# Recurrence and token mixing on one core: four-token rows for keys and receptances, a two-bank product without drains, a new written order

## The chip, the cores and the metric

The kernel runs on one core of one Trainium2 chip. The metric is the device time of one execution in microseconds. The page of the profile names the engines PE (TensorE products), PEld (its weight loads), DVE (VectorE), ACT (ScalarE), POOL (GpSimd) and SP (SyncE, which issues the DMAs).

## The reference

Two stages follow each other, for 4 batches, 8 heads, 768 tokens and 48 columns a head. Arrays r, k, v, w are [4, 8, 768, 48] in float32; u is [8, 48].

```python
for t in range(S):                      # a recurrence over tokens, one 48x48 state a head
    cur = einsum('bhd,bhe->bhde', u[None] * kt, vt)          # the bonus of the token itself
    y[:, :, t] = einsum('bhd,bhde->bhe', rt, state + cur)
    state = wt[:, :, :, None] * state + einsum('bhd,bhe->bhde', kt, vt)
...
x = y as [4, 768, 384]
W_tok = scale * einsum('bsd,btd->bst', x @ w_q, x @ w_k)     # w_q, w_k: [384, 64]
out = maximum(einsum('bst,btd->bsd', W_tok, x), 0) @ w_out   # w_out: [384, 384]
```

## The kernel before, in words

The 768 tokens of a batch are cut into chunks of 128 tokens (C) and the work into units of two chunks (U = 256 tokens, all 8 heads). There are N = 12 units, three a batch. A unit loads its decays (wg), keys (kg), receptances (rg) and values (vg), 384 KB each, with `load` (L299): a partition holds two neighbouring tokens of every head, so a row in DRAM that is moved at a time is 2 x 48 floats, 384 bytes, and one DMA fills 128 partitions. For the last batch (WHOLE) the values of all three units come through `load_whole` (L304) in four DMAs of 64 partitions with rows of 192 bytes.

Within a unit the steps are these; the names in brackets are the tiles of the profile.

- ScalarE takes the logarithm of the decays (lw); GpSimd or ScalarE casts keys and receptances to bf16 (k, r), GpSimd the values (v).
- PE sums the logarithms over the tokens of a chunk with a triangle of ones (CM); ScalarE makes exp of the sum (ep, `f_ep` L497, one instruction a unit) and of its negative (en, `f_en` L502). In the first and the last unit this goes chunk by chunk.
- PE transposes keys and receptances (`transposed` L513). VectorE or ScalarE copies the transposed keys (ks); VectorE makes receptances times ep (RT) and receptances times keys (qT). Keys times en (KT, `f_KT` L550) is GpSimd's, except in the first and last unit, where VectorE reads the keys from PSUM.
- The values go through PE to put the tokens of a chunk on the partitions in the order of the transposed keys (v times PM or ID16), and are copied (VB). With the bonus vector UB a product gives a number a token and head (dd), GpSimd multiplies it into the values (Vd).
- Within a chunk: KT times RT (PE), times a mask on VectorE (AM, 128x1024, once a chunk), times VB (`f_ya`).
- Between chunks: keys transposed back (kd), the state of a head pair grown on PE and scaled on VectorE (SB), and RT times the old state, `f_yi` (L717). [...] The step goes in "sides": first the even heads of chunk 0 with the odd heads of chunk 1, then the other two, and ahead of a second side stands a drain of PE:

```python
sides = [[(0, 0), (1, 1)], [(1, 0), (0, 1)]]      # pairs (chunk, odd or even head)
...
if not first:
    nc.tensor.drain()
```

- Both results of a chunk lie in one PSUM bank; VectorE scales by gx and adds Vd in one instruction for the two chunks (X, `f_x` L751).
- X is transposed (XT) and multiplied by w_q and w_k (QK). After the third unit of a batch, T sums keys times X over the tokens, and each unit of the batch is finished: QK times TS, relu (MX), times w_out (wo), copy (os), store.

All PSUM is one tile of eight banks. `unit` (L436) does not issue instructions; it adds steps to `Plan` with an engine or a choice of engines, a duration in ns, the steps it comes after, and the buffers that it fills and reads. `Plan.order` (L86) walks these steps as a list scheduler: on each engine they stand by a written rank (RANK, L171), choices between engines come from a string (ALT, L205), and a PSUM bank is chosen where a buffer comes free. The program is issued in the order that comes out; nothing reorders it later. Loads go to SP's queue in that order; rings of four tiles for wg, kg, rg and vg hold them, so a load waits until the cast of the unit four before it is done. `mm` (L247) is the helper through which every product goes, so all PE instructions stand on L248 in the profile; `copy` is on L391 to L399.

Of the kernel before, what the change touches and what calls it, by code (L numbers as in the profile page):

```python
# [10 lines left out]
F32 = mybir.dt.float32  # L11
# [12 lines left out]
class Buf:  # L24


    def __init__(self, kind):
        self.kind = kind
        self.readers = []
        self.filler = None  # L30
        self.bank = None


class Plan:
# [3 lines left out]
    SWITCH = 93  # L38
    LAND = 1950

    def __init__(self, rings, alt):
        self.rings = rings
        self.alt = iter(alt)
        self.last = {}
        self.steps = []

    def add(self, key, engs, fn, after=(), buf=None, reads=(), lag=None, mode=0, behind=None):
        opts = {}
        for e, x in engs.items():
            x = x if isinstance(x, tuple) else (x, mode, None)  # L50
            own = (260 if e in "Ee" else 80) if lag is None else lag
            opts[e] = (e.upper(), x[0], own, x[1], x[2])
        e = next(iter(opts)) if len(opts) == 1 else next(self.alt, "")
        e = e if e in opts else next(iter(opts))
        eng, dur, own, mode, kind = opts[e]
        if kind is not None:
            buf.kind = kind
        s = dict(key=key, opts=opts, way=e, eng=eng, dur=dur, fn=fn, lag=own, mode=mode, rank=0,
                 behind=behind, after=list(after), buf=buf, reads=list(reads), i=len(self.steps))
        if buf is not None:  # L60
            if buf.filler is None:
                buf.filler = s
                s["fill"] = buf.kind
                if behind is None:
                    s["behind"] = self.last.get(buf.kind)
                if buf.kind in self.rings:
                    self.last[buf.kind] = s
            else:
                s["fill"] = None
                if behind is None:  # L70
                    s["behind"] = buf.filler
        else:
            s["fill"] = None
        for b in reads:
            b.readers.append(s)
        self.steps.append(s)
        return s

    def dma(self, key, issue, dur, fn, after=(), buf=None, reads=(), behind=None):

        i = self.add(key, {"S": issue}, fn, after, buf, lag=0, behind=behind)
        m = self.add(key + ("wire",), {"Q": dur}, None, [i], lag=0)
        l = self.add(key + ("land",), {"L": self.LAND}, None, [m], lag=0, reads=reads)
        return i, l

    def order(self):  # L86
        never = 1 << 60
        queues = {e: [] for e in "EADPS"}
        for s in sorted(self.steps, key=lambda s: s["rank"]):
            if s["eng"] in queues:  # L90
                queues[s["eng"]].append(s)
        wires = {}
        for s in self.steps:
            if s["eng"] in "QL":
                wires.setdefault(s["after"][0]["i"], s)
        free = dict.fromkeys("EADPSQ", 0)
        place = dict.fromkeys("EADPS", 0)
        rings = {k: [] for k in self.rings}
        owners, moved, done, mode = [None] * 8, [], [], 0

        def clear(b):
            if b is None:
                return 0
            return max([x.get("end", never) for x in b.readers], default=0)

        def start(s):
            if any("end" not in a for a in s["after"]):
                return never, None
            t = max([free[s["eng"]]] + [a["end"] for a in s["after"]])
            if s["behind"] is not None:  # L110
                if "start" not in s["behind"]:
                    return never, None
                t = max(t, s["behind"]["start"])
            if s["eng"] == "S" and len(moved) >= 3:
                t = max(t, moved[-3])
            if s["fill"] in ("w", "s"):
                two = s["fill"] == "w"
                at = [clear(x) for x in owners]
                end = 7 if two else 8
                t = max(t, min(max(at[x:x + 1 + two]) for x in range(end)))  # L120
                if t >= never:
                    return never, None

                def beside(x):
                    return (x > 0 and at[x - 1] <= t) + (x < end - 1 and at[x + 1 + two] <= t)
                x = min((x for x in range(end) if max(at[x:x + 1 + two]) <= t),
                        key=lambda x: (beside(x), x if two else -x))
                return t, (x, 1 + two)
            if s["fill"] is not None:
                ring, size = rings[s["fill"]], self.rings[s["fill"]]  # L130
                if len(ring) >= size:
                    t = max(t, clear(ring[-size]))
            return t, None

        def run(s, t, took):
            s["start"], s["end"] = t, t + took + s["lag"]
            free[s["eng"]] = t + took
            done.append(s)

        while True:  # L140
            heads = [(start(q[place[e]]), e) for e, q in queues.items() if place[e] < len(q)]
            if not heads:
                break
            (t, at), e = min(heads, key=lambda h: h[0][0])
            assert t < never, "the plan is stuck"
            s = queues[e][place[e]]
            place[e] += 1
            if at is not None:
                s["buf"].bank = at[0]
                for x in range(at[0], sum(at)):  # L150
                    owners[x] = s["buf"]
            elif s["fill"] is not None:
                rings[s["fill"]].append(s["buf"])
            change = e == "E" and s["mode"] != mode
            if e == "E":
                mode = s["mode"]
            run(s, t, s["dur"] + self.SWITCH * change)
            if s["i"] in wires:
                m = wires[s["i"]]
                run(m, max(free["Q"], s["end"]), m["dur"])  # L160
                moved.append(free["Q"])
                x = wires[m["i"]]
                x["start"], x["end"] = m["end"], m["end"] + x["dur"]
                done.append(x)
        assert len(done) == len(self.steps)
        return done

RANK = [  # L171
# [40 lines left out]
def kernel(  # L212
# [24 lines left out]
    HW = H * D2  # L237
    N = B * NU

    WHOLE = (3,)  # L240
    DIRECT = (0, N - 1)

    SHIFT = 25
# [690 lines left out]
```

## Time and profile before

| | |
|---|---|
| runs | 106.45, 120.07, 106.38 us; median 106.45 |
| profiled execution, span | 104.5 us, from its first to its last instruction; mean granted clock 0.955 |
| busy PE, DVE, ACT, POOL | 88.3, 81.7, 81.0, 69.8 us |
| DMA | 24.68 MB in 56805 packets, 54480 of them under 512 bytes |
| granted clock of PE | half from 20.1 to 26.9 us and in the last 2 us |
| first load landed, waited for by ACT | 4.47 us |
| cast of the last receptances (POOL) | 79.43 us |
| last transposes of receptances on PE | 81.41 us |
| last product on PE begins / last store issued | 97.28 us (a run of 15, 2.60 us) / 100.8 us |

The page's second part cuts the span into 40 slices of 2.6 us. A line of the groups gives line, engine, operation, tiles and shape, the count, then busy us and the mean ns of one, then the idle time of the engine just ahead of them and who ended it. "issue" means that nothing which the profile shows ended a wait. In the chain in order of time each line has start, length and what ran; SPq is the issuing of a DMA on SP.

### The profile page before, as it was taken

The page shows a single profiled execution, that of the slowest core. Times are in us where ns is not written, and L with a number is a line of the kernel's source. Part 1 is how long each engine was busy: PE and PEld are TensorE (multiplying, and loading weights), DVE is VectorE, ACT ScalarE, POOL GpSimd, SP SyncE. Part 2 cuts the span into 40 slices and gives each one's busy share as a digit, 9 for nine tenths or more (in the row PEclk, how much of TensorE's full clock was granted, in tenths as well). Part 3 has the DMA queues.
Part 4 walks back from the last instruction along what each step waited for, and adds up shares of the span by engine and source line. Part 5 has one row for each costly group of instructions (what it writes and reads, how often), then busy time and mean ns, then how long its engine had stood idle before and what let it go on. Part 6 is the DMA issues. An engine that isn't in the chain of part 4 may idle for free.

```text
span 104.5 us, 4513 instructions
## 1 busy us (share of the span) xinstructions
PE 88.3 (84%) x1913; PEld 65.1 (62%) x1916; DVE 81.7 (78%) x139; ACT 81.0 (78%) x123; POOL 69.8 (67%) x80
## 2 busy tenths in 40 slices
PE   5966985589878898999899999699999999999920
PEld 2243754478756676586667777477788668866600
DVE  6628989765899797988889979989999898864500
ACT  6256999568889976987998988979889778666930
POOL 6667395998699977996876999994899506000000
PEclk9999999855899999999999999999999999999995
DMA  1999998999899999999999999999960019303792
GB/s 19 295 324 325 325 321 222 267 239 319 194 335 276 244 245 252 294 262 288 301 274 280 310 306 266 170 197 231 307 220 8 6 65 391 153 9 152 295 365 94
DMA packets 56805, 24.68 MB, mean 236 GB/s; under 512 B 54480, under 2 KB 55632, under 8 KB 56784
## 3 DMA queue, kind: packets, MB, share of 16 engines
q1 hardware_dynamic: 56224, 24.19, 83.9%
q8 instruction: 15, 0.25, 0.9%
q10 hardware_dynamic: 560, 0.20, 0.7%
q14 instruction: 6, 0.05, 0.2%
HBM read 19.66 MB, written 4.72 MB: 233 GB/s over the span
## 4 chain that ended last, share of the span: by engine, by line
PE 53%; DVE 15%; SPq 10%; DMA 6%; issue 4%; POOL 3%; ACT 3%; DVEq 0%; POOLq 0%; ACTq 0%
PE PS L248 53%; SPq L300 10%; DVE AM L636 6%; DMA kg<-in_k_dram 6%; DVE X L752 3%; DVE ks L397 3%; POOL KT L558 2%; ACT os L391 2%; POOL k L470 1%; ACT MX L403 1%; ACT VB L391 1%; DVE SB L694 1%; DVE qT L534 1%; DVE RT L548 1%; DVE XT L397 1%
## 5 line engine op out<-in xcount | busy, mean ns | idle before, releaser
L636 DVE TENSOR_TENSOR AM<-PS,US 128x1024 bf16<-128x1024 f32 x24 | 29.2, 1219 | 1.0 <-PE PS L248 0.8
L558 POOL TENSOR_TENSOR KT<-ks,en 128x1024 bf16<-128x1024 bf16 x9 | 19.1, 2127 | 5.4 <-DVE ks L397 2.4
L616 POOL TENSOR_TENSOR Vd<-VB,dd 128x768 bf16<-128x768 bf16 (+1 forms) x14 | 18.5, 1327 | 5.5 <-DVE AM L636 4.3
L752 DVE SCALAR_TENSOR_TENSOR X<-PS,gx,Vd 128x768 bf16<-128x768 f32 (+1 forms) x13 | 12.4, 953 | 2.3 <-PE PS L248 1.8
L498 ACT ACTIVATE ep<-PS 128x1024 bf16<-128x1024 f32 (+1 forms) x14 | 12.8, 922 | 1.8 <-PE PS L248 1.7
L248 PE MATMUL PS<-wo,MX 128*128 128x384 bf16 x72 | 13.2, 326 | 0.0
L503 ACT ACTIVATE en<-PS 128x1024 bf16<-128x1024 f32 (+1 forms) x14 | 12.5, 903 | 0.7 <-issue 0.4
L460 ACT ACTIVATE lw<-wg 128x768 bf16<-128x768 f32 x12 | 10.2, 847 | 2.9 <-DMA wg<-in_w_dram 2.9
L470 POOL CAST k<-kg 128x768 bf16<-128x768 f32 x12 | 9.9, 822 | 2.9 <-DMA kg<-in_k_dram 2.9
L248 PEld LDWEIGHTS <-KT 48*128 48x128 bf16 (+1 forms) x320 | 9.4, 95 | 3.4 <-issue 1.4
L391 ACT COPY os<-PS 128x768 f32<-128x768 f32 (+1 forms) x14 | 9.5, 684 | 1.4 <-PE PS L248 1.3
L403 ACT ACTIVATE MX<-PS 128x768 bf16<-128x768 f32 (+1 forms) x11 | 8.3, 754 | 2.4 <-PE PS L248 2.3
L248 PE MATMUL PS<-RT,KT 48*128 48x128 bf16 x192 | 9.7, 220 | 0.5 <-POOL KT L558 0.4
L548 DVE TENSOR_TENSOR RT<-PS,ep 128x1024 bf16<-128x1024 bf16 (+1 forms) x14 | 8.4, 609 | 1.7 <-PE PS L248 1.6
L248 PEld LDWEIGHTS <-MX 128*128 128x128 bf16 x72 | 6.5, 98 | 4.0 <-issue 0.2
L470 POOL CAST r<-rg 128x768 bf16<-128x768 f32 x10 | 8.2, 823 | 1.1 <-DMA rg<-in_r_dram 1.1
L391 ACT CAST VB<-PS 128x768 bf16<-128x768 f32 x9 | 7.2, 800 | 2.1 <-PE PS L248 2.0
L534 DVE TENSOR_TENSOR qT<-PS,ks 128x1024 bf16<-128x1024 bf16 x12 | 8.2, 684 | 0.7 <-PE PS L248 0.7
L248 PE MATMUL PS<-SB,RT 48*128 48x48 bf16 x160 | 6.9, 184 | 2.1 <-DVE AM L636 0.9
L248 PE MATMUL PS<-VB,AM 128*128 128x48 bf16 x192 | 8.7, 186 | 0.0
L579 POOL CAST v<-vg 128x768 bf16<-128x768 f32 x9 | 7.4, 824 | 1.8 <-DMA vg<-in_v_dram 1.8
L248 PE MATMUL PS<-CM,lw 64*128 64x128 bf16 x192 | 8.4, 232 | 0.2
(83 smaller groups left out, 188.1 us busy)
## 6 DMA issues: line engine op xcount, KB each, us to landing
wg<-in_w_dram SPq DMA_DIRECT2D x12, 384.0 KB, 5.5
kg<-in_k_dram SPq DMA_DIRECT2D x12, 384.0 KB, 5.6
rg<-in_r_dram SPq DMA_DIRECT2D x12, 384.0 KB, 5.8
vg<-in_v_dram SPq DMA_DIRECT2D x9, 384.0 KB, 5.4
out_dram<-os SPq DMA_DIRECT2D x9, 384.0 KB, 3.6
vw<-in_v_dram SPq DMA_DIRECT2D x4, 288.0 KB, 5.9
out_dram<-os SPq DMA_DIRECT2D x5, 192.0 KB, 2.5
wof<-in_moe_w_out_dram SPq DMA_DIRECT2D x1, 576.0 KB, 6.0
```

Source lines behind the costliest of these rows:

```text
L248: return nc.tensor.matmul(o, l, rr, start=start, stop=stop, skip_group_check=True, is_transpose=trans)
L300: nc.sync.dma_start(out=view(tl, 0, [[D2, H], [1, D2]]), in_=ap[b, :, ds(i * U, U)].rearrange("h (p j) d -> p h (j d)", j=2))
L391: nc.scalar.copy(o, i)
L460: nc.scalar.activation(view(lw.tile, 0, [[64, H], [512, 2], [1, D]]), view(g["wg"].tile, 0, [[D2, H], [D, 2], [1, D]]), ACT.Ln, bias=0.0, ...
L470: op(view(o.tile, 0, [[64, H], [512, 2], [1, D]]), view(g[src].tile, 0, [[D2, H], [D, 2], [1, D]]))
L498: nc.scalar.activation(view(ep.tile, cs[0] * NP * EW + 66, [[EW, NP * len(cs)], [-65, 2], [1, 64]]), at(cw)[:, ds(cs[0] * 512, w_)], ACT.E ...
L503: nc.scalar.activation(en.tile[:, ds(cs[0] * 512, w_)], at(cw)[:, ds(cs[0] * 512, w_)], ACT.Exp, bias=0.0, scale=-1.0)
L548: nc.vector.tensor_tensor(o, x, y, ALU.mult)
L558: x.tensor_tensor(o, view(ks.tile, cs[0] * 512, dims), y, ALU.mult)
L616: nc.gpsimd.tensor_tensor(Vd.tile[:, cols], VB.tile[:, cols], view(dd.tile, cs[0] * H, [[1, len(cs) * H], [0, D]]), ALU.mult)
L636: AMs[c] = add(("AM", n, c), {"D": 1221}, lambda e, c=c, A=A: nc.vector.tensor_tensor(view(AM[c].tile, 0, [[C, 8], [1, C]]), view(at(A), 0 ...
L752: nc.vector.scalar_tensor_tensor(view(X.tile, (2 * i + c0) * DM, [[DM, nc_], [1, DM]]), view(at(y), 0, [[512, nc_], [1, DM]]), gx, view(Vd ...
```

## The change

- Keys and receptances of the units 1 to 11 come in rows of four tokens, 768 bytes (`load_long`): 64 partitions hold the 256 tokens of a unit for four heads, the other 64 partitions the other four heads. Each such load is two DMAs of 64 partitions. The values of the last batch come in four DMAs of 32 partitions, rows of 192 bytes as before. Decays and the other values are loaded as before.
- Tokens of a chunk stand in another order: two bits of the token number choose the group of 32. Masks (CM, US, PM), positions, casts, transposes, copies and the order in QK follow. ep is laid out in runs of 32 columns and made by two instructions, each for half the columns.
- The between-chunk product goes chunk by chunk, even and odd head in turn, even heads into one PSUM bank, odd heads into the other. Outside the last unit there is no drain; X is then read bank by bank, in two instructions. The last unit keeps one drain a chunk.
- The bonus vector is loaded in rows and transposed on PE.
- KT may be made by GpSimd, by VectorE from ks or by VectorE from PSUM, in any unit; casts, VB and Vd may go to more engines; the state product has a second form with 64 columns of weights. The pads of kd are steps of the plan; wo is loaded and cast apart from wq and wk.
- The list scheduler goes: ORDER (all 734 steps), WAYS and BANKS are written out.

```diff
+    def order(self):
+        ways = iter(WAYS)
+        for s in self.steps:
+            if len(s["ways"]) > 1:
+                s["way"] = next(ways)
...
+        for b, x in zip(self.banks, BANKS):
+            b.bank = x
...
+        for i in ORDER:
+            s = self.steps[i]
...
-    WHOLE = (3,)
-    DIRECT = (0, N - 1)
+    LONG = tuple(range(1, N))
+    WHOLE = (B - 1,)
...
+    def load_long(b, i, tl, ap):
+        for g in range(2):
+            nc.sync.dma_start(
+                out=view(tl, 0, [[2 * D2, NP], [1, 2 * D2]], p0=64 * g, pn=64),
+                in_=ap[b, ds(g * NP, NP), ds(i * U, U)].rearrange("h (p s) d -> p h (s d)", s=4))
+
     def load_whole(b, q, tl):
...
+        nc.sync.dma_start(
+            out=view(tl, 0, [[D, H * NCH], [1, D]], p0=64 * (q % 2) + 32 * (q // 2), pn=32),
+            in_=dataclasses.replace(v, offset=(b * H * S + q) * D,
+                                    ap=[[4 * D, 32], [C * D, H * NCH], [1, D]]))
...
             def f_ep(e, cs=cs, w_=w_):
-                nc.scalar.activation(
-                    view(ep.tile, cs[0] * NP * EW + 66, [[EW, NP * len(cs)], [-65, 2], [1, 64]]),
-                    at(cw)[:, ds(cs[0] * 512, w_)], ACT.Exp, bias=0.0, scale=1.0)
+                for off, step, j in ((68, 34, 0), (34, -33, 1)):
+                    nc.scalar.activation(
+                        view(ep.tile, cs[0] * NP * EW + off,
+                             [[EW, NP * len(cs)], [step, 2], [1, 32]]),
+                        view(at(cw), cs[0] * 512 + j * 64, [[C, NP * len(cs)], [32, 2], [1, 32]]),
+                        ACT.Exp, bias=0.0, scale=1.0)
...
+                if long:
+                    for hp in range(2):
+                        for s in range(4):
+                            for x in range(2):
+                                rows = ds(x * 64, 64)
+                                mm(at_long(x, place + hp * C + (s % 2) * 64 + (s // 2) * 32),
+                                   src.tile[rows, ds(s * 256 + hp * 128, 128)],
+                                   ID16[rows, rows], trans=True)
+                    return
...
+            y = add(("KT", n, cs[0]), "PDd", f_KT, [ens[c] for c in cs], KT, [en],
+                    cols=512 * len(cs), half=half,
+                    more=dict(P=([kss], [ks]), D=([kss], [ks]), d=([kTs], [kr])))
...
-        if end:
-            sides = [[(0, 0)], [(0, 1)], [(1, 1)], [(1, 0)]]
-        else:
-            sides = [[(0, 0), (1, 1)], [(1, 0), (0, 1)]]
...
+        def of(c, h):
+            return at(ys[c])[:, ds(h * D if end else h % 2 * 512 + (c * NP + h // 2) * D, D)]
+
+        def f_yi(e, c, start):
+            heads = [(hp, hh) for hp in range(NP) for hh in range(2)]
+            if end:
+                heads.sort(key=lambda x: x[1])
+            for x, (hp, hh) in enumerate(heads):
+                if end and x == NP:
+                    nc.tensor.drain()
+                mm(of(c, 2 * hp + hh), RT.tile[ds(hh * 64, D), ds((c * NP + hp) * C, C)],
+                   olds[c].tile[ds(hh * 64, D), ds(hp * D, D)],
+                   start=(start and hp == 0 and not (end and hh)), stop=False)
...
             def f_x(e, c0=c0, nc_=nc_, y=y):
-                nc.vector.scalar_tensor_tensor(
-                    view(X.tile, (2 * i + c0) * DM, [[DM, nc_], [1, DM]]),
-                    view(at(y), 0, [[512, nc_], [1, DM]]), gx,
-                    view(Vd.tile, c0 * DM, [[DM, nc_], [1, DM]]), ALU.mult, ALU.add)
+                for hh in range(2) if not end else ():
+                    nc.vector.scalar_tensor_tensor(
+                        view(X.tile, 2 * i * DM + hh * D, [[D2, H], [1, D]]),
+                        view(at(y), hh * 512, [[D, H], [1, D]]), gx,
+                        view(Vd.tile, hh * D, [[D2, H], [1, D]]), ALU.mult, ALU.add)
...
```

In SP's queue the first loads stand, before, as w0 k0 r0 v0 k1 w1 r1 v1 w2 r2 k2 v2 (the number is the unit), and after as w0 k0 r0 v0 k1 w1 r1 v1 w2 k2 r2 v2, where k1, r1, k2, r2 are two DMAs each.

More of the change, by code (lines that the diff above doesn't have):

```diff
@@ L24, with __init__, add @@
 class Buf:
-    def __init__(self, kind):
+    def __init__(self, kind, tile=None):
         self.kind = kind
-        self.readers = []
+        self.tile = tile
         self.filler = None
+        self.before = None
         self.bank = None
 class Plan:
[L38 to L44, printed above, removed]
-        self.steps = []
[L47 to L59, printed above, removed]
+    ENGINE = dict(E="E", e="E", c="E", A="A", D="D", d="D", P="P", S="S", Q="Q", L="L")
+    def __init__(self):
+        self.steps = []
+        self.banks = []
+    def add(self, key, ways, fn, after=(), buf=None, reads=(), cols=0, mode=0, behind=None,
+            half=-1, more=None):
+        s = dict(key=key, ways=ways, way=ways[0], fn=fn, after=list(after), buf=buf,
+                 reads=list(reads), cols=cols, mode=mode, behind=behind, half=half,
+                 more=more or {}, i=len(self.steps), fills=False, out=False)
         if buf is not None:
@@ L62, in add @@
                 buf.filler = s
[L63 to L67, printed above, removed]
-            else:
[L69 to L75, printed above, removed]
+                s["fills"] = True
@@ L76, in add @@
+                if buf.tile is None:
+                    self.banks.append(buf)
+                elif behind is None and buf.before is not None:
+                    s["behind"] = buf.before.filler
+            elif behind is None:
+                s["behind"] = buf.filler
         self.steps.append(s)
         return s
[L79 to L84, printed above, removed]
@@ L86, in order @@
-    def order(self):
[L87 to L92, printed above, removed]
-        for s in self.steps:
[L94 to L137, printed above, removed]
-            done.append(s)
[L140 to L165, printed above, removed]
-        return done
@@ L171 @@
-RANK = [
[32 rows of a table removed]
-]
-ALT = ("PPDEAAADeAAPADPeAAeAeAAPPDPeAAAEADAAAAAAAPADPEAAeAEDAPPADEAAEDEDAPPDPeAADEDAAAAAAAAPPAPe"
-       "ADEAeAAPPDPEAAEAEDAPPDPeAAAEDAAAAAAAAPPDPAeAEAAPPAPAEDeADPPAAAEDDDEDDAADDDAADAAADAA")
+    def order(self):
+        ways = iter(WAYS)
+        for s in self.steps:
+            if len(s["ways"]) > 1:
+                s["way"] = next(ways)
+                assert s["way"] in s["ways"], s["key"]
+            s["eng"] = self.ENGINE[s["way"]]
+        for b, x in zip(self.banks, BANKS):
+            b.bank = x
+        assert sorted(ORDER) == list(range(len(self.steps)))
+        done = []
+        for i in ORDER:
+            s = self.steps[i]
+            assert all(x["out"] for x in s["after"]), s["key"]
+            if s["buf"] is not None and s["buf"].kind == "x":
+                s["buf"].kind = "s" if s["way"] == "E" else "w"
+            s["out"] = True
+            done.append(s)
+        return done
@@ L559, in unit @@
[L559 to L567 removed]
+            half = -1 if long or len(cs) > 1 else cs[0]
@@ L679, in f_sn @@
                 x = at(sn)
-                if old is not None:
-                    mm(x[:, ds(0, NP * D)], IDU, old.tile, start=True, stop=False)
+                for o in range(2 if e == "c" else 1) if old is not None else ():
+                    rows = ds(o * 64, 64) if e == "c" else ds(0, 128)
+                    mm(x[rows, ds(0, NP * D)], IDU[:, rows], old.tile, start=True, stop=False)
                 for hp in range(NP):
@@ L684, in f_sn @@
                         h = 2 * hp + hh
[L685 to L689 removed]
+                        k0 = 64 + (c * H + h) * 128
+                        v_ = VB.tile[:, ds(c * DM + h * D, D)]
@@ L732, in unit @@
[L732 to L742 removed]
+        yis, yas = {}, {}
@@ L744, in unit @@
+        for c in range(2):
+            if c not in yas:
+                y_add(c)
         if "X" not in batch:
```

435 lines of the change are left out of this document (218 added, 217 removed), and 78 rows, old and new, of tables (BANKS, ORDER, RANK).

## The prediction

> **What bounds the kernel now.** I read the busy line and the chain of the page first, then the engines by window, then the chain in order of time, then the groups that the change touches. The profiled execution has a span of 104.5 us; the runs' median is 106.45 us, so 1.95 us lie around the span. All sums below are made on the span, and the 1.95 us are added at the end.
>
> ```profile
> PE 88.3 (84%) x1913; PEld 65.1 (62%) x1916; DVE 81.7 (78%) x139; ACT 81.0 (78%) x123; POOL 69.8 (67%) x80
> ...
> PE 53%; DVE 15%; SPq 10%; DMA 6%; issue 4%; POOL 3%; ACT 3%; DVEq 0%; POOLq 0%; ACTq 0%
> ```
>
> No engine is full, and the chain lies for half its length on PE. The windows (busy us of PE, PEld, DVE, ACT, POOL, then granted clock, DMA share, GB/s) say why:
>
> ```profile
> 5.00:10.00 5.00, 3.29 (x64) 1.97 (x64) 2.44 (x6) 2.97 (x7) 3.04 (x5) 1.00 1.17 323
> 10.00:70.00 60.00, 52.00 (x1291) 39.91 (x1294) 52.06 (x75) 50.95 (x73) 51.24 (x47) 0.94 1.04 270
> 64.50:70.20 5.70, 4.68 (x144) 3.62 (x140) 5.20 (x8) 4.91 (x8) 5.70 (x6) 1.00 1.01 192
> 72.00:78.00 6.00, 5.89 (x127) 4.66 (x122) 5.95 (x9) 5.56 (x10) 4.40 (x4) 1.00 0.94 283
> ```
>
> From 10 to 70 us four engines are busy 51 to 52 us of 60 each, and the DMA engines move 270 GB/s where the same loads ran at 323 GB/s from 5 to 10 us. So the middle is a balance: each engine idles 8 to 9 us waiting for another, and the loads are held back now and then by rings that are not yet free (SP's waits in the load phase sum to 19.8 us). In the last 30 us PE is bound: it is 5.89 of 6.00 us busy, and behind the last unit's receptance transposes (81.41 us) its products run to 99.88 us almost without a gap. Only the beginning is bound by loads:
>
> ```profile
> 10.44 1.33 SPq L300
> 11.77 0.04 issue
> 11.81 5.96 DMA kg<-in_k_dram
> ...
> 18.79 0.65 PE PS L248 x24
> 19.45 0.00 issue
> 19.45 0.54 POOL v L579
> 19.98 0.25 issue
> 20.24 2.14 POOL KT L558
> ```
>
> The chain's first 17.8 us are SP's issues and the landing of the third unit's keys, which are the 11th load in SP's list.
>
> **The parts, one by one.**
>
> *Drains.* Before, each unit's between-chunk product (f_yi) runs in two sides with a drain ahead of the second; PE's list has 13 such drains, after it 2 (the last unit's). The price is in the weight loads of that product:
>
> ```profile
> L248 PEld LDWEIGHTS <-RT 48*128 48x128 bf16 x160 | 4.8, 95 | 4.9 <-issue 4.8
> ```
>
> Those 4.8 us of idle time fall in 17 gaps, 0.28 us each, and nothing that the profile shows ended them. 11 drains x 0.28 = 3.1 us of PE. Where PE is on the chain (53%) this is worth 3.1 x 0.53 = 1.6 us; bounds 0 (all on idle PE time) and 3.1. The products stay (160 before and after).
>
> *Start of the queue.* SP's new list issues the third unit's keys as the 10th load, not the 11th: one load earlier, 1.2 us (SP's 1.15 to 1.33 us an issue). Two of the loads ahead of it and that load itself become pairs of half-size transfers, and their pace is the unknown of this change. From below: the nearest long rows are the stores, 3072-byte rows, whose slice of the page reads 391 GB/s: 0.393 MB / 391 = 1.0 us a pair, against 0.393 / 323 = 1.22 now. From above: the only half-partition loads in the trace are the whole-batch values (load_whole, 64 partitions, 192-byte rows), 192 GB/s: 2.05 us. By row length 768 bytes stand between 384 (323 GB/s) and 3072; by partitions they stand with the slow row. I take 1.22, no change, because the slow row has rows a quarter as long; so -1.2 us here, bounds -1.8 and +1.3. Issuing is no limit: SP's first two issues, with nothing queued, took 0.44 and 0.57 us, so a pair costs about 1 us of SP.
>
> *Rest of the loads.* At 1.0 us a pair the 22 pairs would save 4.8 us of DMA time. I count nothing, because the middle does not wait for it: 45 loads of 0.393 MB and 0.79 MB of weights at 323 GB/s are 57.2 us, the values of the last batch 6.1, and 63.3 us stand in the 75.5 us between the first bytes and the last landing (near 78 us). 12 us of slack cover it; the price if the pairs are slower is the first rival.
>
> *X in two halves (f_x).* 11 instructions of 1015 ns become 22 of 384 elements; the 384-element form of before is 614 ns. 2 x 614 - 1015 = +0.21 us a unit, 2.3 us of VectorE. On the chain X stands three times (2.9%): +0.6 us; bounds 0.4 and 2.3. *ep in two halves (f_ep):* 616 ns for 512 elements against 1044 for 1024: +0.19 us, 14 times, 2.6 us of ScalarE, which is 3% of the chain: 0, hidden by PE, and 2.6 if that cover is gone.
>
> ```profile
> L752 DVE SCALAR_TENSOR_TENSOR X<-PS,gx,Vd 128x768 bf16<-128x768 f32 x11 | 11.2, 1015 | 1.9 <-PE PS L248 1.4 <-POOL Vd L616 0.4
> L752 DVE SCALAR_TENSOR_TENSOR X<-PS,gx,Vd 128x384 bf16<-128x384 f32 x2 | 1.2, 614 | 0.4 <-PE PS L248 0.4
> L558 POOL TENSOR_TENSOR KT<-ks,en 128x1024 bf16<-128x1024 bf16 x9 | 19.1, 2127 | 5.4 <-DVE ks L397 2.4 <-issue 1.8 <-ACT ks L391 1.2
> ```
>
> *Engines anew.* GpSimd loses two KT products (2.13 us each on it, 0.69 on VectorE), casts and parts of Vd: 69.8 us becomes about 64. VectorE gains X, two KT, three casts (bounds 0.55 and 1.0 us, the bf16 and the fp32 copy rows), VB and other copies, and loses others: +4.8 us in all, +3 of it ahead of the last unit. ScalarE: ep, two ks copies and so on, +4.3 us. PE's list has the same products but for their order; the single bonus transpose, two more whole-bank kb steps and the half-column state products are each under 0.3 us, both ways.
>
> *The order.* It cannot be costed edit by edit. PE idles 8.0 us from 10 to 70 us: no order wins more than that, and one as bad as that is good would lose as much. PE's own waits for GpSimd's keys and KT are 2.7 us; I take a third of them away, -0.9 us, since GpSimd loses 8% of its work and the second unit's KT leaves it. This is a choice, and it is the softest term.
>
> **Sum.** -1.6 -1.2 +0.6 -0.9 = -3.1: 101.4 us of span, and with the 1.95 us around it **103.3 us**. Its own range is 101.4 to 105.0.
>
> **Rivals.**
>
> *Half-partition loads set the pace (slower).* If a pair goes as the values of the last batch do, 22 x (2.05 - 1.22) = 18.3 us more DMA time. 12 us of it fall into the slack; the last receptances land 6.3 us later. Their transposes then come at 87.7 us instead of 81.4, with 18.5 us of PE behind them, of which about 3 us (products of the batch before) will by then have been done, and 4.6 us to the end: 107.8 + 1.95 = 109.8 us. It decides from 1.22 + 12 / 22 = 1.77 us a pair. For it speaks the 192 GB/s window, against it that these rows are 192 bytes long. [...]
>
> *VectorE and ScalarE bind.* They run 52 of 60 us in the middle. If their idle share stays (0.868 busy), +3 us of VectorE ahead of the tail cost 3.5 us, against -1.2 at the start and -1.6 of drains: 104.5 + 0.7 + 1.95 = 107.1 us.
>
> *The order closes half of PE's idle time in the middle.* -4.0 in place of -0.9: 98.3 + 1.95 = 100.2 us. For it: KT products come earlier where VectorE makes them; against it: the tail, PE at 98%, has no such room.
>
> *Nothing of it arrives:* drains removed where PE waits anyway, the keys' load no earlier: 106.5 us.
>
> **Chances.** Forecast 0.42, better order 0.18, VectorE and ScalarE 0.20, half-partition loads 0.17, nothing 0.03. Two per cent, about what a measurement of this kernel can tell from no change, are 104.3 and 108.6 us. Faster: most of the forecast (0.38) and the better order, 0.56. Within: the rest of the forecast, 0.14 of the second rival, the 0.03: 0.21. Slower: the loads and the upper part of the second rival, 0.23. The range 100.2 to 109.5 leaves out a little at both ends, chiefly the loads at their full price.
>
> **What would show it.** Right: idle time ahead of the RT weight loads near 1 us; X twice at about 0.61 us; GB/s of 300 and more where pairs run; the last receptances cast before 78 us; PE at 98% from there on. Wrong: SP's issues of pairs at 0.9 us and more each through the middle with the DMA share near 1 and GB/s near 200, ScalarE and GpSimd waiting for kg and rg (the loads' rival); VectorE over 9 tenths in every slice from 10 to 80 us with PE waiting for it (the second); the same PE gaps elsewhere (the drains bought nothing).

## The result, and the profile after

The changed kernel takes 113.34 us (median of 112.57, 113.15, 113.54 and 113.93), the kernel before, run beside it, 106.51 us. The ratio is 1.065, with a 95% interval of 1.060 to 1.070: slower by 6.8 us, where 3.1 us less had been forecast. The profiled execution has a span of 112.1 us. Some executions of a kernel run a per cent or more slower than its others, as the 120.07 us of the kernel before; the ratios here and below leave them out, the medians do not, and the profiles of experiments 1, 2, 3 and 6 are of such executions.

First the page's busy line, its granted clock and bandwidth by slices (2.8 us each), and the chain:

```profile
PE 92.8 (83%) x1908; PEld 67.9 (61%) x1908; DVE 84.8 (76%) x152; ACT 82.8 (74%) x141; POOL 64.8 (58%) x78
...
PEclk9999855555599999999999999985999999999999
...
GB/s 46 323 321 265 293 243 276 146 284 226 257 229 230 251 243 283 227 220 231 252 257 239 231 225 210 251 178 182 204 244 389 62 6 200 229 0 103 282 347 118
...
PE 31%; DMA 28%; SPq 18%; POOL 9%; issue 4%; ACT 4%; DVE 3%; POOLq 0%; DVEq 0%
```

DMA holds 28% of the chain where it held 6%, SP's issuing 18% where it held 10%, and PE fell from 53% to 31%. From the fourth slice on, where pairs run, the bandwidth is mostly below 260 GB/s. Four windows of the kernel after follow, then the last two of them for the kernel before (the prediction shows its first two; the columns are again PE, PEld, DVE, ACT, POOL, clock, DMA share, GB/s):

```profile
5.00:10.00 5.00, 4.03 (x82) 2.73 (x82) 4.36 (x13) 3.32 (x10) 1.95 (x4) 1.00 1.17 305
10.00:70.00 60.00, 51.13 (x1150) 38.64 (x1144) 49.93 (x81) 47.88 (x73) 40.06 (x37) 0.86 1.09 241
70.00:78.00 8.00, 4.72 (x105) 3.19 (x101) 4.45 (x7) 3.74 (x7) 4.55 (x5) 0.80 1.07 204
78.00:84.00 6.00, 5.83 (x159) 4.57 (x158) 5.20 (x9) 5.38 (x10) 5.12 (x4) 0.99 1.07 222
```

```profile
70.00:78.00 8.00, 7.75 (x193) 6.28 (x190) 7.92 (x11) 7.56 (x12) 6.21 (x6) 1.00 0.93 259
78.00:84.00 6.00, 5.89 (x131) 4.54 (x130) 5.30 (x10) 4.92 (x8) 4.45 (x5) 1.00 0.03 9
```

From 10 to 70 us the DMA engines are more of the time busy (share 1.09 against 1.04) and move less (241 GB/s against 270). That is 29 GB/s x 60 us = 1.7 MB that is missing at 70 us; at the 222 GB/s of the last window it takes 7.8 us to bring. From 70 to 78 us every engine starves, PE included, and from 78 to 84 us, when the kernel before had no loads left, loads still run. Who waits for them is in the waits (us in total, times, longest); first of the kernel after, then of the kernel before:

```profile
POOL k L418 <- DMA kg<-in_k_dram: 10.8, 5, 4.0
POOL r L418 <- DMA rg<-in_r_dram: 7.6, 5, 3.2
ACT lw L407 <- DMA wg<-in_w_dram: 6.4, 5, 2.6
...
POOL r L421 <- DMA rg<-in_r_dram: 1.5, 1, 1.5
...
POOL v L333 <- DMA vg<-in_v_dram: 1.4, 3, 0.7
```

```profile
ACT lw L460 <- DMA wg<-in_w_dram: 2.9, 2, 1.9
POOL k L470 <- DMA kg<-in_k_dram: 2.9, 4, 1.2
...
POOL v L579 <- DMA vg<-in_v_dram: 1.8, 4, 0.6
...
POOL r L470 <- DMA rg<-in_r_dram: 1.1, 2, 0.9
...
ACT r L470 <- DMA rg<-in_r_dram: 0.2, 1, 0.2
```

The casts' and logarithms' waits for loads went from 8.9 to 28.5 us in sum (0.8 of the latter is VectorE's wait for receptances, not shown). The decays and values, whose loads were not changed, come late with the rest: 7.8 us of these 28.5. One piece of the chain in order of time (start, length) shows such a wait whole:

```profile
65.29 0.33 SPq L238
65.62 0.06 issue
65.68 0.60 SPq L238
66.28 0.06 issue
66.34 0.60 SPq L238
66.94 0.04 issue
66.98 6.41 DMA kg<-in_k_dram
73.39 0.05 issue
73.44 0.84 POOL k L418
74.28 0.05 issue
74.33 4.17 PE PS L179 x87
```

SP issues pair after pair on L238, the second half of unit 9's keys lands 6.4 us later, GpSimd casts at once, and PE, which stood idle for 3.28 us, transposes at once. Nothing but the load is on the way. The receptances' weight loads, by their tile (duration, first and last start), date the delay, before and after:

```profile
L248 PEld LDWEIGHTS <-r x192: 92/95/129, 8.0 to 81.6; 64*128 64x128 bf16 x192
```

```profile
L179 PEld LDWEIGHTS <-r x192: 92/95/129, 7.5 to 89.6; 64*128 64x128 bf16 x192
```

The last one starts 8.0 us later, and the span is 7.6 us longer. By unit the lateness of the first of them is +0.9 us in unit 1, +2.7 in unit 2, +0.2 in unit 4, +4.2 in unit 6, +6.6 in unit 9 and +7.9 in unit 11. Between these two kernels the written order differs too. Against experiment 1 below, which differs from the kernel after in the loads alone, the lateness is 3.0 us in unit 2, 4.4 in unit 4, 3.8 in unit 6, 7.8 in unit 9 and 9.1 in unit 11: some of it is made good at times, but it grows over the run and is not the fault of one place.

### The profile page after: what moved, and what is told of

It is laid out like the page before. It is cut to its first block, busy times and chain, and to the rows that moved or that the text cites. A ratio compares the mean times of both kernels' runs of the same rounds, so it can differ in the third digit from the quotient of the medians.

```text
span 112.1 us, 4538 instructions
## 1 busy us (share of the span) xinstructions
PE 92.8 (83%) x1908; PEld 67.9 (61%) x1908; DVE 84.8 (76%) x152; ACT 82.8 (74%) x141; POOL 64.8 (58%) x78
## 4 chain that ended last, share of the span: by engine, by line
PE 31%; DMA 28%; SPq 18%; POOL 9%; issue 4%; ACT 4%; DVE 3%; POOLq 0%; DVEq 0%
PE PS L179 31%; DMA rg<-in_r_dram 11%; DMA kg<-in_k_dram 10%; SPq L238 10%; SPq L232 8%; DMA vg<-in_v_dram 7%; POOL KT L534 3%; POOL v L333 2%; POOL r L418 1%; POOL k L418 1%; POOL Vd L583 1%; DVE X L718 1%; ACT ks L327 1%; ACT MX L339 1%; ACT XT L327 1%
## 5 line engine op out<-in xcount | busy, mean ns | idle before, releaser
L583 POOL TENSOR_TENSOR Vd<-VB,dd 128x768 bf16<-128x768 bf16 (+1 forms) x13 | 17.2, 1328 | 2.9 <-ACT dd L327 2.8
L534 POOL TENSOR_TENSOR KT<-ks,en 128x1024 bf16<-128x1024 bf16 (+1 forms) x8 | 16.1, 2009 | 2.1 <-DVE ks L333 1.2
L418 POOL CAST k<-kg 128x768 bf16<-128x768 f32 x11 | 9.1, 825 | 12.4 <-DMA kg<-in_k_dram 10.8
L179 PEld LDWEIGHTS <-KT 48*128 48x128 bf16 (+1 forms) x304 | 10.9, 100 | 5.4 <-DVE KT L529 1.7
L718 DVE SCALAR_TENSOR_TENSOR X<-PS,gx,Vd 128x384 bf16<-128x384 f32 x22 | 12.5, 609 | 2.2 <-PE PS L179 2.1
L447 ACT ACTIVATE ep<-PS 128x512 bf16<-128x512 f32 (+1 forms) x28 | 13.4, 549 | 0.1
L666 DVE TENSOR_TENSOR SB<-PS,ep 128x192 bf16<-128x192 f32 x20 | 7.0, 352 | 5.1 <-PE PS L179 4.7
L327 ACT COPY ks<-PS 128x1024 bf16<-128x1024 bf16 x6 | 6.1, 1016 | 5.2 <-PE PS L179 5.2
L179 PE MATMUL PS<-Z 128*128 128x512 bf16 x21 | 8.9, 532 | 1.2 <-DVE Z L250 1.2
L179 PEld LDWEIGHTS <-lw 64*128 64x128 bf16 x192 | 6.6, 105 | 4.3 <-ACT lw L407 3.3
L179 PE MATMUL PS<-ID,k 64*128 64x64 bf16 x176 | 5.1, 199 | 4.5 <-POOL k L418 3.3
```

The lines of the kernel that those rows point to most:

```text
L179: return nc.tensor.matmul(o, l, rr, start=start, stop=stop, skip_group_check=True, is_transpose=trans)
L327: nc.scalar.copy(o, i)
L418: op(view(o.tile, 0, [[64, NP], [256, 4], [1, D]]), view(g[src].tile, 0, [[2 * D2, NP], [D, 4], [1, D]]))
L447: nc.scalar.activation(view(ep.tile, cs[0] * NP * EW + off, [[EW, NP * len(cs)], [step, 2], [1, 32]]), view(at(cw), cs[0] * 512 + j * 64, ...
L534: x.tensor_tensor(KT.tile[:, cols], ks.tile[:, cols], en.tile[:, cols], ALU.mult)
L583: (nc.vector if e == "D" else nc.gpsimd).tensor_tensor(Vd.tile[:, cols], VB.tile[:, cols], view(dd.tile, cs[0] * H, [[1, len(cs) * H], [0, ...
```

## The experiments

All twelve stand in this table; each is explained below. GB/s is the window from 10 to 70 us; the last column but one is when the last weight load of receptances starts, the last the span of the profiled execution less that. The ratio is to the kernel before, run on the same chip; those of the last two rest on one and on two executions and have no interval. Experiment 2 reads other tokens than the reference and stands there for its time alone.

| kernel | median us | ratio (95%) | GB/s | last r | rest of span |
|---|---|---|---|---|---|
| before | 106.5 | 1 | 270 | 81.6 | 22.9 |
| after | 113.3 | 1.065 (1.060 to 1.070) | 241 | 89.6 | 22.5 |
| 1 after, two-token rows | 104.0 | 0.975 (0.967 to 0.983) | 264 | 81.0 | 22.4 |
| 2 after, long rows on 128 partitions | 101.6 | 0.951 (0.943 to 0.959) | 290 | 79.0 | 22.5 |
| 3 before, loads in partition halves | 114.8 | 1.076 (1.068 to 1.084) | 243 | 91.1 | 23.3 |
| 4 before, loads in halves by heads | 106.2 | 1.004 (0.994 to 1.014) | 274 | 80.5 | 23.2 |
| 5 after, four DMAs of one row | 254.4 | 2.40 (2.38 to 2.41) | | | |
| 6 as 1, with 11 drains | 104.6 | 0.983 (0.975 to 0.992) | 265 | 82.0 | 22.3 |
| 7 as 1, r2 before k2 | 103.1 | 0.970 (0.963 to 0.977) | 271 | 78.8 | 22.7 |
| 8 after, PE kept busy | 114.0 | 1.070 (1.060 to 1.079) | 240 | 89.2 | 22.1 |
| 9 after, pairs in units 1 to 5 | 109.4 | 1.022 (1.010 to 1.033) | 253 | 84.5 | 22.3 |
| 10 after, pairs in units 6 to 11 | 110.5 | 1.035 (1.026 to 1.043) | 254 | 86.0 | 22.5 |
| 11 after, halves on two queues | 121.4 | 1.11 | 240 | 94.4 | 22.6 |
| 12 as 1, with 36 drains | 108.6 | 1.007 | 266 | 83.0 | 23.1 |

Behind the last receptances stand 22 to 23 us in every kernel. What a load costs is thus seen in one number: when the last receptances reach PE.

### 1. The rows undone alone

```diff
-    LONG = tuple(range(1, N))
+    LONG = ()
```

> The changed kernel with one part undone: keys and receptances of all units come in two-token rows of 384 bytes, one DMA over 128 partitions, as before the change (the set LONG is empty; casts, transposes and copies follow as they do for the first unit); the written order, the two banks, X and ep in halves stay. Theory 'half partitions' (a DMA that writes 64 partitions only runs at some 240 GB/s against 323, 1.64 us a pair against 1.22, and this is what the 6.8 us come from, with the PE clock that halves where PE waits for loads): 103 to 106 us, 300 GB/s and more in slices without the last batch's values, waits for kg, rg, wg together under 10 us (27 in the changed kernel), half clock no longer than 8 us ahead of 80 us. Theory 'order' (the written order and the halved instructions cost it, the loads are only late because their rings come free late): 110 us or more.

It took 103.98 us; the time of 'half partitions' came, that of 'order' did not. The waits for keys, receptances and decays are 10.8 us (27.1 in the kernel after), a little above the 10 expected; the half clock takes some 7 us ahead of 70 us (mean clock 0.76 from 5 to 10 us and 0.96 from 10 to 70). The bandwidth is above 300 GB/s in some slices only, as in the kernel before. The four-token rows thus cost 9.4 us, and the rest of the change is a gain of 2.4 us over the kernel before.

### 2. The same rows on 128 partitions

```diff
     def load_long(b, i, tl, ap):
-        for g in range(2):
-            nc.sync.dma_start(
-                out=view(tl, 0, [[2 * D2, NP], [1, 2 * D2]], p0=64 * g, pn=64),
-                in_=ap[b, ds(g * NP, NP), ds(i * U, U)].rearrange("h (p s) d -> p h (s d)", s=4))
+        h0, t0 = ((0, 0), (NP, 0), (0, U))[i]
+        nc.sync.dma_start(
+            out=view(tl, 0, [[2 * D2, NP], [1, 2 * D2]]),
+            in_=ap[b, ds(h0, NP), ds(t0, 2 * U)].rearrange("h (p s) d -> p h (s d)", s=4))
```

> The changed kernel, but a load of keys or receptances in units 1 to 11 is one DMA over 128 partitions with the same 768-byte rows, 4 a partition, the same bytes. It reads other tokens (512 tokens of four heads), so what is computed is not the reference; everything else is the changed kernel's. Theory 'half partitions': the row of 768 bytes is as good as or better than 384, a load takes 1.1 to 1.25 us, 102 to 105 us in all. Theory 'long rows' (the 768-byte packet itself is slower for its bytes, 52 ns by the median where 36 lie on the line through the other sizes): no change in the packet's time, 111 to 114 us. Theory 'order': 110 us or more.

It took 101.55 us, a little under the range of 'half partitions'. The 768-byte packets of the trace take 36 ns by the median here and 52 ns in the kernel after; in the quarter microseconds in which hardly anything else moves, about 331 GB/s here and 240 there, that is 1.19 and 1.64 us for 0.393 MB. The row of 768 bytes is not slow: it is better than the one of 384, and worth 2.4 us against experiment 1. The window from 10 to 70 us says it in one line:

```profile
10.00:70.00 60.00, 55.78 (x1339) 42.87 (x1334) 56.42 (x90) 54.16 (x84) 46.49 (x43) 0.89 1.08 290
```

At nearly the DMA share of the kernel after (1.08 against 1.09) it moves 290 GB/s, not 241, and VectorE, of which the prediction feared that 52 of 60 us was its limit, is busy 56.42.

### 3 and 4. The kernel before, its loads cut in two

```diff
+        split = ap is not w and ap is not v and (b, i) != (0, 0)
+        for g in range(2) if split else ():
+            nc.sync.dma_start(
+                out=view(tl, 0, [[D2, H], [1, D2]], p0=64 * g, pn=64),
+                in_=ap[b, :, ds(i * U + g * C, C)].rearrange("h (p j) d -> p h (j d)", j=2))
```

> The kernel before, but keys and receptances of units 1 to 11 come in two DMAs, one for the lower 64 partitions and one for the upper 64, rows of 384 bytes as before; nothing else is changed. Theory 'half partitions': the packets of these loads take longer, 1.5 to 1.7 us a pair; 22 x 0.4 us = 9 us more DMA time, part of it in the slack of 12 us: 108 to 113 us. Theory 'long rows': 106 to 107 us, as before. Theory 'order': 106 to 107 us.

In the other the two DMAs each fill 128 partitions, with half of the heads:

```diff
+                out=view(tl, g * NP * D2, [[D2, NP], [1, D2]]),
+                in_=ap[b, ds(g * NP, NP), ds(i * U, U)].rearrange("h (p j) d -> p h (j d)", j=2))
```

> The kernel before, but keys and receptances of units 1 to 11 come in two DMAs that each write all 128 partitions, one for four heads and one for the other four; rows of 384 bytes. It has as many DMAs as the changed kernel, without half partitions. Theory 'half partitions': 106 to 107.5 us, as before. Theory 'number of DMAs' (88 issues on SP or their fixed cost set the pace): as slow as with the two halves of the partitions, 108 us or more.

114.77 and 106.18 us. The same bytes, the same rows of 384 bytes, the same number of DMAs: cut by partitions they cost 8.4 us, a little more than the range expected; cut by heads nothing. The first of these lines is of the kernel cut by partitions, the second of the one cut by heads:

```profile
10.00:70.00 60.00, 49.26 (x1178) 37.35 (x1176) 47.70 (x68) 46.73 (x67) 46.32 (x42) 0.91 1.14 243
```

```profile
10.00:70.00 60.00, 52.33 (x1328) 40.17 (x1329) 52.69 (x76) 51.81 (x74) 52.13 (x48) 0.97 1.07 274
```

Together with experiment 2 this leaves neither the length of the row nor the number of DMAs as a cause: what costs is that one DMA covers 64 partitions.

### 5. Four DMAs of one row a partition

```diff
+        for hp in range(NP):
+            nc.sync.dma_start(
+                out=view(tl, hp * 2 * D2, [[1, 2 * D2]]),
+                in_=dataclasses.replace(ap, offset=((b * H + hp) * S + i * U) * D,
+                                        ap=[[NP * S * D, 2], [4 * D, 64], [1, 4 * D]]))
```

> The changed kernel, its loads of keys and receptances cut another way: not two DMAs of 64 partitions with four rows each, but four DMAs of 128 partitions with one 768-byte row each (one head for the lower, one for the upper 64 partitions). The layout in SBUF and the result are the changed kernel's. Theory 'half partitions': packets back at 36 to 40 ns, the last receptances issued before 72 us, 101.5 to 104 us in all, near the variant with long rows over 128 partitions. Theory 'issue' (88 issues of 0.45 to 0.6 us, 50 us of SP, are the next bound): 105 to 109 us, with the DMA share well under 1.

254.41 us: neither theory. The packets are back at 36 ns, as 'half partitions' had it, but there are too few at a time. In the page's slices (6.3 us each) the bandwidth sits near 47 GB/s or its double:

```profile
GB/s 197 92 100 108 94 46 105 95 103 47 47 129 64 189 48 46 180 48 47 101 49 47 157 96 100 102 47 102 47 46 46 87 187 60 49 211 18 191 124 253
```

In such a stretch a packet of 768 bytes starts every 16.5 ns and takes 36, so two are under way. The source's slowest dimension is 2 here, where it is 64 or 128 in the other kernels' loads of keys and receptances; two under way fits that, but no run tests this dimension by itself. Another cut that keeps the changed kernel's layout and fills 128 partitions was not tried.

### 8. PE kept busy while it waits

```diff
+HOLD = {("cw", 1): 3, ("rT", 1): 6, ("cw", 2): 5, ("kT", 9): 22}
...
+                for _ in range(HOLD.get((name, n), 0)):
+                    mm(at(kr)[:, ds(place // 2, 256)], Z[:, ds(0, C)], Z[:, ds(0, 256)])
```

> The changed kernel with products of zeros added on PE where it waits for a load: 3 and 5 of 512 columns ahead of the sums of the logarithms of the units 1 and 2, 6 of 256 columns ahead of the receptances of unit 1, 22 of 256 columns ahead of the keys of unit 9 (3.28 us of waiting there). They need no load. Theory 'clock of its own' (the halved clock behind these waits, 17 and 3.4 us long, is a cost beside the late loads): the half-clock stretches go or shrink and 1.5 to 3.5 us with them, 109.8 to 111.8. Theory 'loads alone' (the loads set the end whatever the clock is): 113 to 113.5 us.

The kernel after runs at half clock from 13.3 to 30.4 us and, behind the wait of 3.28 us for unit 9's keys, from 74.75 to 78.16 us. Its windows there:

```profile
74.00:74.50 0.50, 0.17 (x12) 0.18 (x14) 0.00 (x0) 0.00 (x0) 0.50 (x2) 1.00 0.76 141
74.50:75.00 0.50, 0.50 (x40) 0.50 (x34) 0.00 (x0) 0.00 (x0) 0.50 (x1) 0.75 1.16 223
75.00:78.00 3.00, 3.00 (x53) 1.93 (x48) 1.90 (x4) 2.14 (x3) 3.00 (x4) 0.50 1.04 180
78.00:78.50 0.50, 0.50 (x9) 0.49 (x7) 0.50 (x2) 0.10 (x1) 0.50 (x1) 0.84 1.29 212
```

With the products of zeros the clock stays whole at both places:

```profile
10.00:30.00 20.00, 15.26 (x355) 10.35 (x357) 16.16 (x26) 14.42 (x23) 10.45 (x11) 1.00 1.12 245
70.00:78.00 8.00, 7.86 (x178) 6.14 (x177) 5.77 (x9) 5.49 (x10) 5.29 (x6) 1.00 1.06 210
```

(Two stretches of 3.4 us are left, at 30 and at 61 us.) The mean clock is 0.969, in the kernel after 0.909, so 13 us less at half clock, and the time does not move: 113.95 us, 1.070 against 1.065 with intervals that overlap. The waits for loads sum to 26.6 us, where they were 28.5: in sum the engines wait for the loads nearly as long. The added products have a small price of their own (ahead of unit 9's keys they end 0.5 us after the cast), so a gain of that size could hide. The 1.5 to 3.5 us of 'clock of its own' are not there.

### 9 and 10. Half of the pairs

```diff
-    LONG = tuple(range(1, N))
+    LONG = tuple(range(1, 6))        # the tenth: tuple(range(6, N))
```

> The changed kernel with the pairs of half-partition loads in the units 1 to 5 only (10 pairs); the units 6 to 11 load 128 partitions in 384-byte rows. Theory 'slack' (the prediction's step: 12 us of DMA time are free, so 10 pairs at some 0.5 us more, 5 us, are hidden): 103 to 104.5 us, as with no pairs. Theory 'no slack' (the DMA engines are busy from 5 us to the last landing, so each pair's price shows; 9.4 us for 22 pairs are 0.43 us each): 108.2 us.

> The changed kernel with the pairs in the units 6 to 11 only (12 pairs); the units 1 to 5 load 128 partitions in 384-byte rows. Theory 'slack': 103 to 104.5 us. Theory 'no slack': 12 x 0.43 us, 109.1 us.

109.41 and 110.51 us: 'no slack' in both. Against experiment 1, by the ratios times 106.5 us, they are 4.9 us for 10 pairs and 6.3 us for 12, about 0.5 us a pair; all 22 cost 9.5 us, 0.43 each. Even pairs that end with unit 5, with the loads of six units behind them, are not made good. Each is a little over 1 us above its price by 'no slack', and the two together (11.2) are more than all at once (9.5); the intervals of the four ratios are wide enough for that.

### 11. The two halves at once

```diff
-            nc.sync.dma_start(
+            (nc.scalar if g else nc.sync).dma_start(
                 out=view(tl, 0, [[2 * D2, NP], [1, 2 * D2]], p0=64 * g, pn=64),
```

> The changed kernel, the lower half of each pair issued by SP, the upper half by ScalarE at the same place of the written order, so that both can be under way at once. Theory 'one after the other' (the price is that at any time only one half of the partitions is written): the halves now overlap, the 768-byte packets go back towards 36 to 40 ns, and the time falls to 103 to 108 us, unless ScalarE is held by its issues. Theory 'shared engines' (the halves cannot overlap whatever queue they come from): packets at 50 ns and more, 113 us or worse.

121.4 us, and 'shared engines' by the packets: 54 ns by the median. In the ten quarter microseconds in which packets of both queues and hardly others moved, the two halves took about 100 GB/s each and 220 moved in all; in the few in which only one half was written, it was about 226. So it is not that one half waits for the other. Of the time itself part is ScalarE's, which stands still at its issues (43.67 us busy from 10 to 70 us, 47.88 in the kernel after), so the 121.4 us are no measure of the halves.

### 6, 7 and 12. Drains, and the start of the queue

The sixth puts a drain ahead of the second chunk's product, 11 in all, the twelfth two into every chunk's, 36 in all, both in the kernel of experiment 1:

```diff
+            if not end and c == 1:
+                nc.tensor.drain()
```

```diff
             for x, (hp, hh) in enumerate(heads):
-                if end and x == NP:
+                if (end and x == NP) or (not end and x % 4 == 0):
                     nc.tensor.drain()
```

> The changed kernel with two-token rows (the first experiment's), with one drain of PE put back a unit, ahead of the second chunk's between-chunk product; nothing else. By the prediction's step a drain costs 0.28 us of PE, 11 of them 3.1 us of PE time, of which 1.6 us shows: 105 to 106 us against 104.0. If the drains stood only on idle PE time: 104.0, no change. If the whole price shows: 107.

> The changed kernel with two-token rows and 36 drains of PE, two in each chunk's between-chunk product (the sixth experiment has 11). By the prediction's 0.28 us each, 10 us of PE and at 53% of the chain 5 us more than without: 109 us. By the idle time that the 11 drains added ahead of the weight loads there, (3.2 - 1.6) / 11 = 0.15 us each: 5.2 us of PE, 2.8 us more at 53%: 106.5 us. If drains lie on idle time: 104.

They took 104.64 and 108.56 us. The weight loads of this product in experiments 1, 6 and 12 (busy, mean ns, then the idle time ahead of them):

```profile
L179 PEld LDWEIGHTS <-RT 48*128 48x128 bf16 x160 | 3.9, 93 | 1.6 <-issue 1.2
```

```profile
L179 PEld LDWEIGHTS <-RT 48*128 48x128 bf16 x160 | 4.4, 99 | 3.2 <-issue 3.1
```

```profile
L179 PEld LDWEIGHTS <-RT 48*128 48x128 bf16 x160 | 5.1, 96 | 8.5 <-issue 8.5
```

The 36 drains add 6.9 us of idle time, 0.19 us each. To the time they add about 3.4 us (1.007 less 0.975, times 106.5), 0.1 us each: about half shows. Eleven would then be 1.0 us; the sixth's 0.9 us (0.983 less 0.975) has an interval that holds this and nothing at all, so for 11 alone the size is not settled.

The seventh swaps two loads in SP's list, the third unit's receptances ahead of its keys.

> The changed kernel with two-token rows, with one swap in SP's list: the third unit's receptances ahead of its keys, as before the change. By the prediction's step, the keys one load later at the start cost 1.2 us: 105.2 against 104.0. If the start is not bound by them: 104.0.

103.08 us, 0.970 against 0.975 of experiment 1, the intervals overlapping. A loss of 1.2 us for the later keys is not there; which of the two orders is better is not settled. Experiments 1, 6 and 7 are the versions that compute the reference and beat both kernels.

## Why the prediction was wrong

*The pace of a pair* was the step that failed first: "I take 1.22, no change, because the slow row has rows a quarter as long". Measured, a pair takes about 1.6 us. The reason was true of the slow row and said nothing about the pair. The values' packets of 192 bytes take 15 ns by the median, over 64 partitions in the kernel before and over 32 in the kernel after, and 15 ns lie on the line through the packets of 384 bytes (22 ns), of 768 bytes on 128 partitions (36) and of 1536 (65). At 15 ns a packet 16 engines move 205 GB/s, and that load's window had 192. So that row was slow for its short rows and held no price for 64 partitions; packets of 768 bytes on 64 partitions take 52 ns (experiment 2), and experiments 3 and 4 show that the number of DMAs is not the reason. The prediction had half-partition loads as its first rival, with the right cause and a chance of 0.17, but took its price from the same row, which is slow for another reason. Loads of these rows over 64 partitions moved about 240 GB/s, over 128 about 331 (experiment 2), and two half loads at once 220 where one alone moved 226 (experiment 11). Why the half loads are slower the runs do not show.

*"12 us of slack cover it"* was the second step, and the worse, for even at 1.6 us a pair it would have called the change free (the rival was to decide from 1.77). It divided all bytes by the best rate and called the rest free. But the rings are four tiles deep: a load starts when the cast four units ahead is done, and that cast waits for its own load. What looked like slack in the 75 us would then be waiting on both sides of this loop; that reading is argued from the code. The trace of the kernel after has both sides (between 3 and 82 us SP waits 9.6 us in sum for steps of GpSimd, and over the run GpSimd waits 21.3 us for keys, receptances and values), but the loop was not tried by itself. Shown is that there was none to use: in experiments 9 and 10 ten or twelve pairs show at about 0.5 us each. It holds for the gain too: the prediction counted faster loads at nothing, "because the middle does not wait for it", and experiment 2 gains 2.4 us by them.

*The rival's price*, 109.8 us, was too low by 3.5 us although its pair was too dear (2.05). On the span of the profiled execution it is 4.3 us, 112.1 against 107.8. The last receptances' transposes were to start at 87.7 us and started at 89.3; the other part is the tail: about 3 us of it were to be done by then. They were not. PE is busy 17.81 us behind the last of these weight loads, and 17.91 us in the kernel before:

```profile
89.65:112.10 22.45, 17.81 (x277) 13.01 (x269) 13.07 (x23) 14.73 (x31) 3.75 (x5) 1.00 0.43 161
```

```profile
81.66:104.50 22.84, 17.91 (x266) 12.73 (x256) 12.91 (x25) 14.12 (x25) 2.41 (x3) 0.95 0.46 174
```

In a written order, products of the batch before stand behind the last receptances whether their data is there or not.

*The rest of the forecast.* Without the slow loads (experiment 1) the time is 103.98 us, where 103.3 was forecast, inside its own range of 101.4 to 105.0. Its terms fare less well than their sum, so this is partly luck. The idle time ahead of the RT weight loads fell from 4.9 to 1.2 us in the kernel after, as told:

```profile
L179 PEld LDWEIGHTS <-RT 48*128 48x128 bf16 x160 | 4.2, 100 | 1.2 <-issue 1.0
```

Of the 1.6 us for the drains, about 1.0 is left by experiment 12's rate. The -1.2 us for the earlier keys is not borne out (experiment 7). An instruction of X and of ep takes what its row said (609 and 606 ns, from 614 and 616). The halves run into each other, so that VectorE is busy with X 1.3 us longer in all (12.5 against 11.2) and ScalarE with ep 0.7 us (13.4 against 12.7), not 2.3 and 2.6. No engine is seen waiting for X, and for ep GpSimd waits once, 0.9 us:

```profile
L718 DVE SCALAR_TENSOR_TENSOR X<-PS,gx,Vd 128x384 bf16<-128x384 f32 x22 | 12.5, 609 | 2.2 <-PE PS L179 2.1
L447 ACT ACTIVATE ep<-PS 128x512 bf16<-128x512 f32 x20 | 11.0, 606 | 0.1
L447 ACT ACTIVATE ep<-PS 128x256 bf16<-128x256 f32 x8 | 2.4, 406 | 0.0
```

The -0.9 us of the order and the +0.6 of X were not measured by themselves.

*The rival of VectorE and ScalarE* is out: in experiment 2 they are busy 56.42 and 54.16 of 60 us, so that 52 of 60 was no limit.

*The signs to look for* point to the loads, though not all of the rival's came as named. GpSimd waits for keys and receptances (the two longest lines), but ScalarE waits for decays. The bandwidth is 241 GB/s at a DMA share of 1.09, between the 270 of before and the 200 named. An issue of half a pair takes 0.9 us or more in 15 of 44 cases and 0.6 to 0.8 in the others. Of the signs of being right the idle time ahead of the RT weight loads and X's 0.61 us came; the pace and the early receptances did not (their last cast starts at 87.6 us).

## What to carry to other kernels

Count a load by the partitions that one DMA covers before its rows: the longer row bought a tenth in pace on 128 partitions (290 against 264 GB/s), and the same row on 64 lost nearly as much (241). Time in which the DMA engines are not at their best rate was no slack here, where loads wait for buffers that wait for loads: ten and twelve pairs showed at about 0.5 us each (experiments 9 and 10). Ask instead when the last input reaches the engine that ends the kernel, and what stands behind it. A halved clock cost little here, where its engine would only have waited sooner: 13 us less of it left the time as it was (experiment 8).

## What the runs showed of the hardware that was not expected

- A DMA of 64 partitions was slow also when one on the other half ran beside it: 220 GB/s for both together against about 226 for one alone (experiment 11).
- The median time of a packet ran in a line with its length, where few partitions did not slow it: 192 bytes 15 ns, 384 22, 768 36, 1536 65, and 121 for the stores' 3072 (kernel before, for 768 bytes experiment 2). The rows of 192 bytes over 64 partitions are on it; 768 bytes over 64 partitions are not, with 52 ns (kernel after).
- The DMAs of experiment 5, whose source's slowest dimension is 2, ran two packets at a time, about 47 GB/s.
- The half-clock stretches that end within the trace have lengths of 6.83 us (kernel before, 20.09 to 26.92), 17.07 us and 3.41 us (kernel after, 13.31 to 30.38 and 74.75 to 78.16), which are 2, 5 and 1 times 3.41. In the kernel after PE was busy by the profile through all 3.41 us from 20.14 to 23.55, and the half clock went on to 30.38; what ends such a stretch is left open.
